# Sink keys of a windowed attention: zero-padded full-array matmuls for two heads at once, and one burst of row-tiled score matmuls per unit

## Chip, cores and metric

The kernel runs on one core of one Trainium2 chip. The metric is the device time of one execution in microseconds. A run is called slow when it took over 1.5% more than the fastest of the same kernel in its job, otherwise fast, and only fast runs are compared. Ratios are the mean time of one kernel's fast runs over that of the other's fast runs of the same rounds, so not quite the ratio of the medians that are quoted.

Words used here: PE is TensorE, PEld its weight loads, ACT ScalarE, DVE VectorE, POOL GpSimd. "Start to start" is the distance from the start of one matmul in the trace to the start of the next.

## The reference

Causal attention with a window of 128 keys plus 4 "sink" keys that every query sees, followed by a two-layer FFN.

```python
# B, H, S, D = 4, 8, 768, 64;  n_sink, window = 4, 128
scores = q @ k.T / sqrt(D)
keep = (pos_k < n_sink) | ((pos_q - pos_k >= 0) & (pos_q - pos_k < window))
a = softmax(where(keep, scores, -1e9))
x = (a @ v)  # reordered to (B*S, H*D) = (3072, 512)
h = x @ w_in                                   # 512 -> 2048
out = (h / (1 + exp(-beta * h))) @ w_out       # 2048 -> 512
```

## The kernel before

The program is a list of operations that a small scheduler in Python orders for each engine, with its own model of durations. A *unit* is half a sequence (384 queries) of a pair of heads; there are 32. For each unit: `T` transposes q and k, `SC` computes scores, exps and masks, `AV` multiplies with v (a 65th column of ones gives the denominator), `OT` transposes the result into `xT`. The FFN parts `H` (w_in, 4 matmuls of 384 columns) and `O` (w_out, 16 of 512 columns) fill the gaps.

Blocks of scores are 128 keys by 128 queries. Kinds: `d` diagonal, `p` the block before it, `s` block 0 where it holds both window and sinks, `k` the 4 sink keys alone, for queries too far away to see block 0 in their window. A head has 64 dimensions, so the two heads of a unit lie on rows 0 to 63 and 64 to 127 of the array, and their score matmuls run side by side as row tiles into different PSUM banks.

```python
GROUPS = [[[("s", 0, 0), ("s", 0, 1), ("d", 1, 1), ("p", 1, 2)], [("d", 2, 2), ("k", 0, 2)]],
          [[("d", 3, 3), ("p", 2, 3), ("p", 3, 4)], [("d", 4, 4), ("d", 5, 5), ("p", 4, 5)],
           [("k", 0, 3), ("k", 0, 4), ("k", 0, 5)]]]

def SC(u, j):                       # one group = one burst; two or three per unit
    bs = take(2)                    # two adjacent PSUM banks, one per head
    ...
        for hh in range(2):
            rows = slice(64 * hh, 64 * hh + 64)
            dst = bank[0:NSINK if sink else 128, ...]
            lhsT = kt[rows, 1, 0:NSINK] if sink else kt[rows, 1, kc:kc + 128]
            ... matmul(dst, lhsT, qkT[u % NT][rows, 0, ...])
    ... exp of all of both banks on ACT; masks on POOL and DVE

def AV(u):
    for m, ps in enumerate(parts(half)):        # three blocks of 128 queries
        for hh in range(2):
            for n, (kind, j, i, kb) in enumerate(ps):   # k (sinks) first, then p, d
                rows = slice(0, 128 if kb >= 0 else NSINK)
                ... matmul(A[:, c0:c0 + D + 1], E[z][rows, i, hh, :],
                           vaug[vz][rows, kb % NK, 2 * hp + hh, :], start=(n == 0), ...)
```

The sink scores fill 4 of 128 PSUM rows and the exp reads all 128, so VectorE clears PSUM once at the start (two memsets).

At the start q, k and v arrive per pair of heads. The k loads are issued on ACT's queue, in program order with ACT's casts.

```python
add("act" if hp is not None and n == "k" else "sp", lambda e, ...: e.dma_start(dst, src), ...)
...
LOADS = xl(0) + [0, 1, 2, 3] + xl(1) + [4, 5, 6, 7] + ...   # q,k,v of half 0; w_in; half 1; w_out; the rest
```

The softmax here doesn't subtract the row's maximum and nothing guards it: scores larger than these inputs give would overflow.

## Time and profile before

Median 290.97 us of three runs (289.66 to 291.53). The profiled execution took 287.25 us, its span from first to last instruction 285.5 us.

| | before |
|---|---|
| PE busy | 262.1 us, 92% |
| ACT, DVE, POOL busy | 60%, 45%, 34% |
| PE waiting for a named engine | 20.2 us in all, 15.8 of them for the first q and k casts |
| AV (480 matmuls): busy, its two shapes added / start to start | 62.7 us / 44.3 us |
| changes of array shape between neighbouring matmuls | 386 |

Lines of the profile's page: the busy time of each engine, and over 40 equal slices the busy share of PE and its granted clock in tenths.

```profile
PE 262.1 (92%) x1953; PEld 143.5 (50%) x1953; DVE 128.2 (45%) x252; ACT 172.4 (60%) x280; POOL 97.2 (34%) x192
PE   0249997989999999999999999999999999999995
PEclk9999999798999999999999999999999999999999
PE 86%; ACT 4%; DMA 4%; SPq 2%; DVE 1%; issue 1%; POOL 0%; DVEq 0%
```

The last line is the chain of waits, share of the span by engine. From the fourth slice on PE is busy for 70% or more of every slice but the last, mostly for over 90%, and the chain runs through it, so PE time saved there is mostly time saved. (The clock row misses the start: until 32.5 us w_in matmuls follow each other at 320 ns, and the transposes before them at 107 ns, twice what they take later, so PE ran at half speed there though the row shows 9.) PE's busy time cannot say how much is saved: matmuls overlap, and a matmul that is held up by its neighbour looks no different in its mean duration. The groups of AV by shape (count, then busy us and mean ns of one) show it:

```profile
L517 PE MATMUL P<-vaug,E 128*128 128x65 bf16 x352 | 37.0, 204 | 0.0
L517 PE MATMUL P<-vaug,E 4*128 4x65 bf16 x128 | 25.7, 201 | 0.4 <-ACT E L474 0.4
```

Both forms last about 200 ns. From the start times of all matmuls in the trace the picture differs. Medians, start to start:

```
128-row AV -> 128-row AV        38 ns
128-row AV -> 4-row AV         129 ns     4-row AV -> 128-row AV       131 ns
H -> H (384 columns)           163 ns     H -> row-tiled scores        258 ns
O -> O (512 columns)           216 ns     O -> row-tiled scores        312 ns
64x128 scores -> H             148 ns     128-column transpose -> same  56 ns
```

Every change of the array's shape adds 91 to 96 ns to the distance seen without it, whichever way. The weight loads show where it is lost: between two 128-row AV matmuls the second one's weight load starts 11 ns after the first matmul (median), but 125 ns after it where the shape changes, 4 ns before its own matmul.

The Trainium skill, "TensorEngine Tiling (Array Packing)", Key Properties, says: "Mode switching requires drain". It gives no time; this trace does.

### The profile page before, as it was taken

How to read it: one execution, taken by the hardware profiler on the slowest of the kernel's cores; microseconds unless marked ns; L12 is line 12 of the kernel's file. 1: busy time of each engine (PE TensorE's matmuls, PEld its weight loads, DVE VectorE, ACT ScalarE, POOL GpSimd, SP SyncE). 2: the span in 40 equal slices, each digit the busy share in tenths (PEclk: the TensorE clock that was granted, in tenths of full speed). 3: DMA queues.
4: the chain of work that ended last, by engine and by line, in shares of the span. 5: the costliest groups of instructions: out<-in, count | busy, mean ns of one | idle time of the engine just before them, and what ended most of it. 6: DMA issues, size and time to landing. Idle time of an engine off the chain costs nothing.

```text
span 285.5 us, 5121 instructions
## 1 busy us (share of the span) xinstructions
PE 262.1 (92%) x1953; PEld 143.5 (50%) x1953; DVE 128.2 (45%) x252; ACT 172.4 (60%) x280; POOL 97.2 (34%) x192
## 2 busy tenths in 40 slices
PE   0249997989999999999999999999999999999995
PEld 0125554444556555565556645555555555555542
DVE  5214694643466463533546523254353353353320
ACT  3359699424786776777867876555555465464430
POOL 2125066665295864949537335000000000000000
PEclk9999999798999999999999999999999999999999
DMA  6962998899999997741000101010010101101001
GB/s 137 279 210 89 307 240 288 240 276 225 275 240 253 229 254 189 181 115 39 1 3 1 39 0 39 0 39 37 37 39 37 65 13 42 68 0 76 37 37 73
DMA packets 82856, 33.89 MB, mean 119 GB/s; under 512 B 75648, under 2 KB 75664, under 8 KB 82832
## 3 DMA queue, kind: packets, MB, share of 16 engines
q1 hardware_dynamic: 79632, 32.78, 42.6%
q10 hardware_dynamic: 3200, 0.79, 1.2%
q8 instruction: 15, 0.25, 0.3%
q14 instruction: 9, 0.07, 0.1%
HBM read 27.27 MB, written 6.29 MB: 118 GB/s over the span
## 4 chain that ended last, share of the span: by engine, by line
PE 86%; ACT 4%; DMA 4%; SPq 2%; DVE 1%; issue 1%; POOL 0%; DVEq 0%
PE P L555 30%; PE P L573 30%; PE P L517 14%; PE P L467 6%; PE P L418 4%; DMA k_stage<-in_k_dram 3%; ACT E L474 2%; PE P L535 2%; SPq L349 2%; DMA q_stage<-in_q_dram 1%; ACT w_in L306 1%; DVE onorm L523 1%; ACT qkT L306 1%; ACT t L559 0%; DVE g L561 0%
## 5 line engine op out<-in xcount | busy, mean ns | idle before, releaser
L561 DVE SCALAR_TENSOR_TENSOR g<-t,P 128x384 bf16<-128x384 f32 x128 | 70.2, 554 | 94.0 <-ACT t L559 82.4
L559 ACT ACTIVATE t<-P,hbeta 128x384 f32<-128x384 f32 x128 | 73.8, 582 | 49.6 <-PE P L555 47.0
L555 PE MATMUL P<-xT,w_in 128*128 128x384 bf16 x512 | 100.8, 331 | 0.1
L573 PE MATMUL P<-w_out,g 128*128 128x512 bf16 x384 | 99.5, 385 | 0.5 <-DVE g L561 0.5
L474 ACT ACTIVATE E<-P 128x768 bf16<-128x768 f32 (+1 forms) x80 | 61.2, 817 | 19.3 <-PE P L467 19.2
L481 POOL TENSOR_SCALAR_AFFINE_SELECT E<-E 128x256 bf16<-128x256 bf16 (+1 forms) x112 | 54.7, 516 | 46.6 <-ACT E L474 46.6
L555 PEld LDWEIGHTS P<-xT,w_in 128*128 128x128 bf16 x512 | 48.5, 99 | 40.4 <-issue 4.6
L573 PEld LDWEIGHTS P<-w_out,g 128*128 128x128 bf16 x384 | 36.0, 99 | 36.3 <-issue 2.9
L517 PE MATMUL P<-vaug,E 128*128 128x65 bf16 (+1 forms) x480 | 46.5, 203 | 0.4 <-ACT E L474 0.4
L517 PEld LDWEIGHTS P<-vaug,E 128*128 128x128 bf16 (+1 forms) x480 | 31.6, 98 | 18.4 <-issue 3.2
L467 PE MATMUL P<-qkT 64*128 64x256 bf16 (+3 forms) x288 | 27.0, 266 | 1.3 <-ACT E L474 1.1
L306 ACT ACTIVATE osb<-P 128x512 f32<-128x512 f32 x22 | 13.1, 597 | 13.8 <-PE P L573 13.6
L306 ACT ACTIVATE xT<-P 128x384 bf16<-128x384 bf16 x26 | 12.6, 494 | 12.7 <-PE P L535 12.6
L489 DVE TENSOR_TENSOR E<-E,maskS 128x512 bf16<-128x512 bf16 x16 | 8.6, 537 | 23.1 <-ACT E L474 23.1
L467 PEld LDWEIGHTS P<-qkT 64*128 64x128 bf16 (+1 forms) x288 | 10.1, 91 | 17.2 <-issue 7.5
L523 DVE TENSOR_TENSOR onorm<-P,rden 128x384 bf16<-128x384 f32 x32 | 17.8, 557 | 1.1
L418 PE MATMUL P<-ident,k_0 128*128 128x128 bf16 x48 | 6.0, 241 | 10.6 <-POOL k_0 L405 10.6
L405 POOL TENSOR_SCALAR_AFFINE_SELECT vaug<-v_stage 128x512 bf16<-128x512 f32 x21 | 14.3, 679 | 3.8 <-DMA v_stage<-in_v_dram 2.4
L306 ACT ACTIVATE qkT<-P 128x768 bf16<-128x768 bf16 x14 | 11.0, 810 | 5.6 <-PE P L418 4.1
L405 POOL TENSOR_SCALAR_AFFINE_SELECT k_0<-k_stage 128x512 bf16<-128x512 f32 (+1 forms) x13 | 7.6, 584 | 17.4 <-DMA k_stage<-in_k_dram 17.4
L535 PE MATMUL P<-ident,onorm 128*128 128x128 bf16 x96 | 11.3, 233 | 1.8 <-DVE onorm L523 1.8
L521 DVE RECIPROCAL rden<-P 128x6 f32<-128x6 f32 x32 | 6.2, 193 | 14.8 <-PE P L517 14.7
(34 smaller groups left out, 98.0 us busy)
## 6 DMA issues: line engine op xcount, KB each, us to landing
out_dram<-osb SPq DMA_DIRECT2D x24, 256.0 KB, 2.0
q_stage<-in_q_dram SPq DMA_DIRECT2D x21, 256.0 KB, 4.3
k_stage<-in_k_dram SPq DMA_DIRECT2D x21, 256.0 KB, 4.3
v_stage<-in_v_dram SPq DMA_DIRECT2D x21, 256.0 KB, 4.3
wst<-in_moe_w_in_dram SPq DMA_DIRECT2D x4, 1024.0 KB, 6.8
wst<-in_moe_w_out_dram SPq DMA_DIRECT2D x4, 1024.0 KB, 6.7
q_stage<-in_q_dram SPq DMA_DIRECT2D x8, 96.0 KB, 2.7
v_stage<-in_v_dram SPq DMA_DIRECT2D x8, 96.0 KB, 2.7
```

Of the source, the lines that this page charges most:

```text
L306: return lambda e: e.activation(dst, src, AF.Copy, bias=0.0, scale=scale)
L405: fn = lambda e: e.affine_select(dst, src, patt, ALU.is_ge, 0.0, base=0, channel_multiplier=0)
L418: add("pe", lambda e, i=i, n=n, c=c: nc.tensor.transpose(mp[:, i * HALF + c * 128:i * HALF + (c + 1) * 128], x16[n][hb % NX][:, c, 2 * hp: ...
L467: add("pe", lambda e, dst=dst, lhsT=lhsT, rows=rows, q0=q0, nq=nq: e.matmul(dst, lhsT, qkT[u % NT][rows, 0, q0:q0 + 128 * nq].rearrange("p ...
L474: add("act", lambda e: e.activation(dst_, src, AF.Exp, bias=0.0, scale=SCALE), act_ns(256 * n), w=[(k_, z, j) for k_ in "Edps"], x=[("B", ...
L481: add("gp", lambda e, d=d, sg=sg, at_=at_: e.affine_select(d, d, [[0, 2 * len(at_)], [sg, 128]], ALU.is_ge, 0.0, base=min(sg, 0), channel_ ...
L517: e.matmul(A[:, c0:c0 + D + 1], E[z][rows, i, hh, :], vaug[vz][rows, kb % NK, 2 * hp + hh, :], start=a, stop=o), mm_ns(D + 1),
L523: add("dve", lambda e: e.tensor_tensor(onorm[on][:, :, :, :].rearrange("p m h d -> p (m h) d"), av[:, :, 0:D], rden[on][:, :].unsqueeze(2) ...
L555: add("pe", lambda e, c=c: e.matmul(hp, w_in16[:, c, m * 128:(m + 1) * 128], xT[:, c, t0:t0 + HALF], start=(c == 0), stop=(c == 3)), mm_ns ...
L559: add("act", lambda e: e.activation(tt[ti][:, :], hp, AF.Tanh, bias=0.0, scale=hbeta[:, m:m + 1]), act_ns(HALF) + 93, r=["hbeta"], w=[("t" ...
L561: add("dve", lambda e: e.scalar_tensor_tensor(gt[T_ % NG][:, m, :], tt[ti][:, :], 1.0, hp, ALU.add, ALU.mult), dve_ns(HALF), r=[("t", ti)] ...
L573: add("pe", lambda e, m=m: e.matmul(P[:, bk, :], gt[T_ % NG][:, m, t * 128:(t + 1) * 128], w_out16[:, m, :], start=(m == 0), stop=(m == NM ...
```

## The change

Its intent: no 4-row matmuls at all, and one row-tiled burst per unit instead of two or three. The sink keys of both heads are copied into one zero-padded stationary tile `kS` (head 0 in columns 0 to 3 of rows 0 to 63, head 1 in columns 32 to 35 of rows 64 to 127), so one full-array matmul `SS` gives both heads' sink scores. The sink values go into `vS`, zero but for rows 0 to 3 (head 0) and 32 to 35 (head 1). A zero score has exp 1, but its row of `vS` is zero. One 130-column matmul then starts the accumulation of both heads.

```diff
-    GROUPS = [[[s0, s1, d1, p(1,2)], [d2, k2]],           [[d3, p3, p4], [d4, d5, p5], [k3, k4, k5]]]
+    GROUPS = [[[s0, s1, d1],         [d2, p(1,2)]],       [[d3, p3, p4], [d4, d5, p5]]]
-    def SC(u, j):                     +    def SC(u):
-        bs = take(2)                  +        bs = take(4)        # both groups, four adjacent banks
...                                    # all matmuls of both groups, then both exps
+        G.free["pe"] += 190           # the scheduler's model learns what a burst costs
+    def SS(u):
+        ... matmul(P[:, bs[0], q0:HALF], kS[ks][:, :], qkT[u % NT][:, 0, q0:HALF])
+        ... exp -> ES[z]
     def AV(u):
         for m, ps in enumerate(parts(half)):
+            far = NK * half + m >= 2
+            if far:
+                matmul(A[:, c0:c0 + 2 * (D + 1)], ES[z][:, m * 128:(m + 1) * 128],
+                       vS[b % 2][:, 2 * hp:2 * hp + 2, :], start=True, stop=False)
             for hh in range(2):
-                    rows = slice(0, 128 if kb >= 0 else NSINK)
-                    ... mm_ns(D + 1)
+                    ... start=(n == 0 and not far) ... 39     # ns in the scheduler's model
     def T(u):       # in the first half of each sequence
+        kS[ks][rows, 32 * hh:32 * hh + NSINK] <- k's first 4 columns in PSUM, for each head
     def cast(...):
+        vS[z][32 * hh:32 * hh + NSINK, ...] <- vaug, on DVE
     def consts():
+        memsets of kS and vS on POOL
-        two memsets of PSUM on DVE
```

(The diff is abridged: block names are shortened, bookkeeping of the scheduler is left out.)

More of the change, by code (lines that the diff above doesn't have):

```diff
@@ L229, in _program @@
     NU = 2 * NPAIR
-    NSTG, NX, NV, NT, NE, NON, NG, NTT, NOS, NWS = 2, 2, 3, 8, 3, 3, 3, 3, 3, 2
+    NSTG, NX, NV, NT, NE, NON, NG, NTT, NOS, NWS, NKS = 2, 2, 3, 8, 3, 3, 3, 3, 3, 2, 4
     NK = NB // 2
@@ L245, in _program @@
     qkT = sb("qkT", (128, 2, HALF), BF16, NT)
-    E = sb("E", (128, 9, 2, 128), BF16, NE)
+    E = sb("E", (128, 6, 2, 128), BF16, NE)
+    ES = sb("ES", (128, HALF), BF16, NE)
+    kS = sb("kS", (128, 128), BF16, NKS)
+    vS = sb("vS", (128, H, D + 1), BF16, 2)
     onorm = sb("onorm", (128, NK, 2, D), BF16, NON)
@@ L316, in consts @@
             add("gp", lambda e, i=i: e.memset(vaug[i][:, :, :, D:D + 1], 1.0), 50, w=[("vones", i)])
+        for i in range(NKS):
+            add("gp", lambda e, i=i: e.memset(kS[i][:, :], 0.0), 80, w=[("kS", i)])
+        for i in range(2):
+            add("gp", lambda e, i=i: e.memset(vS[i][:, :, :], 0.0), 350, w=[("vS", i)])
         for i, sg in ((0, 1), (1, -1)):
@@ L323, in consts @@
             r=[("maskS0", 0), ("maskS0", 1)], w=["maskS"])
-        for h in range(2):
-            add("dve", lambda e, h=h: e.memset(P[:, 4 * h:4 * h + 4, :], 0.0), 2200,
-                x=[("B", i) for i in range(4 * h, 4 * h + 4)])
     def beta_in():
@@ L408, in cast @@
         add(eng, fn, opts[eng], r=r, w=w)
+        if n == "v" and hb % 2 == 0 and (hp == 3 or c == 0):
+            z = hb // 2 % 2
+            v0 = vaug[hb % NV][0:NSINK, 0, :, :].rearrange("p (a two) d -> p a two d", two=2)
+            for hh in range(2):
+                dst_ = vS[z][32 * hh:32 * hh + NSINK, :, :].rearrange("p (a two) d -> p a two d", two=2)[:, :, hh, :]
+                add("dve", lambda e, dst_=dst_, hh=hh: e.tensor_copy(dst_, v0[:, :, hh, :]), 200,
+                    r=[("vS", z)] + [("v", hb % NV, 0, j) for j in range(4)], w=[("vSd", z, hh)])
     def T(u):
@@ L425, in T @@
             w=[("qkT", u % NT)], x=[("B", bs[0])])
+        if hb % 2 == 0:
+            ks = u % NKS
+            for hh in range(2):
+                rows = slice(64 * hh, 64 * hh + 64)
+                add(eng, copy_fn(eng, kS[ks][rows, 32 * hh:32 * hh + NSINK], mp[rows, HALF:HALF + NSINK]), 70,
+                    r=[("kS", ks)], w=[("kSd", ks, hh)], x=[("B", bs[0])])
         give(bs)
-    GROUPS = [[[("s", 0, 0), ("s", 0, 1), ("d", 1, 1), ("p", 1, 2)], [("d", 2, 2), ("k", 0, 2)]],
-              [[("d", 3, 3), ("p", 2, 3), ("p", 3, 4)], [("d", 4, 4), ("d", 5, 5), ("p", 4, 5)],
-               [("k", 0, 3), ("k", 0, 4), ("k", 0, 5)]]]
+    GROUPS = [[[("s", 0, 0), ("s", 0, 1), ("d", 1, 1)], [("d", 2, 2), ("p", 1, 2)]],
+              [[("d", 3, 3), ("p", 2, 3), ("p", 3, 4)], [("d", 4, 4), ("d", 5, 5), ("p", 4, 5)]]]
     def slots(half):
@@ L442, in slots, with SC @@
         return out_
-    def SC(u, j):
+    def SC(u):
         b, half, hp = where(u)
         z = u % NE
-        bs = take(2)
-        grp = GROUPS[half][j]
-        n = len(grp)
-        s0 = slots(half)[grp[0]][1]
-        jobs = {}
-        for i, (kind, kb, qb) in enumerate(grp):
-            jobs.setdefault((kb, kind == "k"), []).append((qb, i))
-        for (kb, sink), cols in jobs.items():
-            cols.sort()
-            own = u if kb >= NK * half else u - 4
-            kt = qkT[own % NT]
-            kc = (kb % NK) * 128
-            q0, i0, nq = (cols[0][0] - NK * half) * 128, cols[0][1], len(cols)
-            st = cols[1][1] - i0 if nq > 1 else 1
-            for hh in range(2):
-                rows = slice(64 * hh, 64 * hh + 64)
-                bank = P[:, bs[hh], :].rearrange("p (s w) -> p s w", w=128)
-                dst = bank[0:NSINK if sink else 128, i0:i0 + st * (nq - 1) + 1:st, :]
-                lhsT = kt[rows, 1, 0:NSINK] if sink else kt[rows, 1, kc:kc + 128]
-                add("pe", lambda e, dst=dst, lhsT=lhsT, rows=rows, q0=q0, nq=nq: e.matmul(
-                    dst, lhsT, qkT[u % NT][rows, 0, q0:q0 + 128 * nq].rearrange("p (s w) -> p s w", w=128),
-                    start=True, stop=True), mm_ns(128 * nq) / 2,
-                    r=[("qkT", u % NT), ("qkT", own % NT)], x=[("B", bs[hh])])
-        step = bs[1] - bs[0]
-        src = P[:, bs[0]:bs[1] + 1:step, 0:128 * n].rearrange("p h (s w) -> p h s w", w=128)
-        dst_ = E[z][:, s0:s0 + n, :, :].rearrange("p s h w -> p h s w")
-        add("act", lambda e: e.activation(dst_, src, AF.Exp, bias=0.0, scale=SCALE), act_ns(256 * n),
-            w=[(k_, z, j) for k_ in "Edps"], x=[("B", i) for i in bs])
-        give(bs)
-        for kind, sg in (("d", 1), ("p", -1)):
-            at_ = [i for i, blk in enumerate(grp) if blk[0] == kind]
-            if at_:
-                d = E[z][:, s0 + at_[0]:s0 + at_[-1] + 1, :, :].rearrange("p s h w -> p (s h) w")
-                add("gp", lambda e, d=d, sg=sg, at_=at_: e.affine_select(
-                    d, d, [[0, 2 * len(at_)], [sg, 128]], ALU.is_ge, 0.0, base=min(sg, 0), channel_multiplier=-sg),
-                    pool_ns(256 * len(at_), 2 * len(at_)), r=[("E", z, j)], w=[(kind, z, j)])
-        if grp[0][0] == "s":
-            d = E[z][:, s0:s0 + 2, :, :]
-            mask = maskS[:, :, :].unsqueeze(2).to_broadcast([128, 2, 2, 128])
-            opts = {"gp": 1150, "dve": dve_ns(512)}
-            eng = quickest(opts)
-            add(eng, lambda e: e.tensor_tensor(d, d, mask, ALU.mult), opts[eng], r=[("E", z, j), "maskS"],
-                w=[("s", z, j)])
@@ new lines, in SC @@
+        bs = take(4)
+        for j, grp in enumerate(GROUPS[half]):
+            jobs = {}
+            for i, (kind, kb, qb) in enumerate(grp):
+                jobs.setdefault(kb, []).append((qb, i))
+            for kb, cols in jobs.items():
+                cols.sort()
+                own = u if kb >= NK * half else u - 4
+                kt = qkT[own % NT]
+                kc = (kb % NK) * 128
+                q0, i0, nq = (cols[0][0] - NK * half) * 128, cols[0][1], len(cols)
+                st = cols[1][1] - i0 if nq > 1 else 1
+                for hh in range(2):
+                    rows = slice(64 * hh, 64 * hh + 64)
+                    bank = P[:, bs[2 * j + hh], :].rearrange("p (s w) -> p s w", w=128)
+                    dst = bank[:, i0:i0 + st * (nq - 1) + 1:st, :]
+                    add("pe", lambda e, dst=dst, kt=kt, kc=kc, rows=rows, q0=q0, nq=nq: e.matmul(
+                        dst, kt[rows, 1, kc:kc + 128],
+                        qkT[u % NT][rows, 0, q0:q0 + 128 * nq].rearrange("p (s w) -> p s w", w=128),
+                        start=True, stop=True), mm_ns(128 * nq) / 2,
+                        r=[("qkT", u % NT), ("qkT", own % NT)], x=[("B", bs[2 * j + hh])])
@@ new lines, in SC @@
+        G.free["pe"] += 190
+        for j, grp in enumerate(GROUPS[half]):
+            n, s0 = len(grp), slots(half)[grp[0]][1]
+            src = P[:, bs[2 * j]:bs[2 * j] + 2, 0:128 * n].rearrange("p h (s w) -> p h s w", w=128)
+            dst_ = E[z][:, s0:s0 + n, :, :].rearrange("p s h w -> p h s w")
+            add("act", lambda e, src=src, dst_=dst_: e.activation(dst_, src, AF.Exp, bias=0.0, scale=SCALE),
+                act_ns(256 * n), w=[(k_, z, j) for k_ in "Edps"], x=[("B", i) for i in bs[2 * j:2 * j + 2]])
+            for kind, sg in (("d", 1), ("p", -1)):
+                at_ = [i for i, blk in enumerate(grp) if blk[0] == kind]
+                if at_:
+                    d = E[z][:, s0 + at_[0]:s0 + at_[-1] + 1, :, :].rearrange("p s h w -> p (s h) w")
+                    add("gp", lambda e, d=d, sg=sg, at_=at_: e.affine_select(
+                        d, d, [[0, 2 * len(at_)], [sg, 128]], ALU.is_ge, 0.0, base=min(sg, 0), channel_multiplier=-sg),
+                        pool_ns(256 * len(at_), 2 * len(at_)), r=[("E", z, j)], w=[(kind, z, j)])
+            if grp[0][0] == "s":
+                d = E[z][:, s0:s0 + 2, :, :]
+                mask = maskS[:, :, :].unsqueeze(2).to_broadcast([128, 2, 2, 128])
+                opts = {"gp": 1150, "dve": dve_ns(512)}
+                eng = quickest(opts)
+                add(eng, lambda e, d=d, mask=mask: e.tensor_tensor(d, d, mask, ALU.mult), opts[eng],
+                    r=[("E", z, j), "maskS"], w=[("s", z, j)])
@@ new lines, in SC @@
+        give(bs)
+    def SS(u):
+        b, half, hp = where(u)
+        z, ks = u % NE, (u - 4 * half) % NKS
+        q0 = 0 if half else 256
+        bs = take(1)
+        add("pe", lambda e: e.matmul(P[:, bs[0], q0:HALF], kS[ks][:, :], qkT[u % NT][:, 0, q0:HALF], start=True,
+                                     stop=True), mm_ns(HALF - q0),
+            r=[("kSd", ks, 0), ("kSd", ks, 1), ("qkT", u % NT)], x=[("B", bs[0])])
+        add("act", lambda e: e.activation(ES[z][:, q0:HALF], P[:, bs[0], q0:HALF], AF.Exp, bias=0.0, scale=SCALE),
+            act_ns(HALF - q0), w=[("ES", z)], x=[("B", bs[0])])
+        give(bs)
@@ L492, in parts @@
     def parts(half):
         sl = slots(half)
-        return [[("E" if blk[0] == "k" else blk[0], sl[blk][0], sl[blk][1], -1 if blk[0] == "k" else blk[1])
-                 for blk in sorted(sl, key=lambda x: "kspd".index(x[0])) if blk[2] == qb]
+        return [[(blk[0], sl[blk][0], sl[blk][1], blk[1])
+                 for blk in sorted(sl, key=lambda x: "spd".index(x[0])) if blk[2] == qb]
                 for qb in range(NK * half, NK * half + NK)]
@@ L501, in av_keys @@
         ks = {(p[0], z, p[1]) for ps in parts(where(u)[1]) for p in ps}
-        return sorted(ks) + [("v", u // 4 % NV, c, u % 4) for c in range(NK)]
+        return sorted(ks) + [("v", u // 4 % NV, c, u % 4) for c in range(NK)] + [("ES", z), ("vSd", u // 8 % 2, 1)]
     def AV(u):
@@ L509, in AV @@
         for m, ps in enumerate(parts(half)):
+            far = NK * half + m >= 2
+            if far:
+                c0 = 2 * m * (D + 1)
+                add("pe", lambda e, m=m, c0=c0: e.matmul(
+                    A[:, c0:c0 + 2 * (D + 1)], ES[z][:, m * 128:(m + 1) * 128],
+                    vS[b % 2][:, 2 * hp:2 * hp + 2, :].rearrange("p h d -> p (h d)"), start=True, stop=False,
+                    skip_group_check=True), mm_ns(2 * (D + 1)),
+                    r=[("ES", z), ("vSd", b % 2, 0), ("vSd", b % 2, 1)], x=[("B", bs[0])])
             for hh in range(2):
@@ L512, in AV @@
                 for n, (kind, j, i, kb) in enumerate(ps):
-                    rows = slice(0, 128 if kb >= 0 else NSINK)
-                    kb = max(kb, 0)
                     vz = (u if kb >= NK * half else u - 4) // 4 % NV
-                    add("pe", lambda e, c0=c0, hh=hh, i=i, kb=kb, vz=vz, rows=rows, a=(n == 0), o=(n == len(ps) - 1):
-                        e.matmul(A[:, c0:c0 + D + 1], E[z][rows, i, hh, :], vaug[vz][rows, kb % NK, 2 * hp + hh, :],
-                                 start=a, stop=o), mm_ns(D + 1),
+                    add("pe", lambda e, c0=c0, hh=hh, i=i, kb=kb, vz=vz, a=(n == 0 and not far), o=(n == len(ps) - 1):
+                        e.matmul(A[:, c0:c0 + D + 1], E[z][:, i, hh, :], vaug[vz][:, kb % NK, 2 * hp + hh, :],
+                                 start=a, stop=o, skip_group_check=True), 39,
                         r=[(kind, z, j), ("v", vz, kb % NK, hp)], x=[("B", bs[0])])
@@ L585, in OQ @@
                 dma=f"do{z}")
-    done = {s: 0 for s in ("cast", "T", "SC", "AV", "OT", "H", "O", "load", "W")}
+    done = {s: 0 for s in ("T", "SC", "SS", "AV", "OT", "H", "O", "load")}
     def xl(hb):
@@ L595, in _program @@
     LOADS = xl(0) + [0, 1, 2, 3] + xl(1) + [4, 5, 6, 7] + [x for hb in range(2, NSB) for x in xl(hb)]
-    SCS = [(u, j) for u in range(NU) for j in range(2 if where(u)[1] == 0 else 3)]
-    n_sc = [0] * (NU + 1)
     CASTS = [x for hb in range(NSB) for x in xl(hb)]
@@ L601, in _program @@
     n_cast, n_w = [0], [0]
-    def units_sc():
-        i = done["SC"]
-        return NU if i == len(SCS) else SCS[i][0]
     def head(s):
@@ L611, in head @@
         if s == "T":
-            if i >= NU or i - NT + 4 >= units_sc():
+            if i >= NU or i - NT + 4 >= min(done["SC"], done["SS"]):
                 return None
@@ L618, in head @@
             fn = lambda: (T(i), mark(("qkTu", i), ("qkT", i % NT)))
-        elif s == "SC":
-            if i >= len(SCS):
-                return None
-            u, j = SCS[i]
-            if u >= done["AV"] + NE:
-                return None
-            t, tb = G.at([("qkTu", u)]), banks_at(2)
-            fn = lambda: SC(u, j)
+        elif s in ("SC", "SS"):
+            if i >= NU or i >= done["AV"] + NE:
+                return None
+            t, tb = G.at([("qkTu", i)]), banks_at(4 if s == "SC" else 1)
+            fn = lambda: (SC if s == "SC" else SS)(i)
         elif s == "AV":
-            if i >= NU or i >= done["OT"] + NON or i >= units_sc() or n_cast[0] < (3 * i + 3 if i < 4 else 12 + 9 * (i // 4)):
+            if i >= NU or i >= done["OT"] + NON or i >= min(done["SC"], done["SS"]) or n_cast[0] < (3 * i + 3 if i < 4 else 12 + 9 * (i // 4)):
                 return None
@@ L714, in _program @@
         best = None
-        for s in ("OT", "AV", "SC", "T") + ffn:
+        for s in ("OT", "AV", "SC", "SS", "T") + ffn:
             h = head(s)
@@ L744, in _program @@
         done[s] += 1
-        if s in "HO":
+        if s in ("H", "O"):
             last = s
```

## The prediction

> **What bounds the kernel.** TensorE. The engine table has PE busy 92% of a 285.5 us span (ACT 60%, DVE 45%, POOL 34%), the chain of waits is 86% PE, and the table of waits shows about 20 us of PE waiting, 16 of them for the first q and k casts before 21 us. From 80 us to the end the stretch view shows PE without gaps. So what PE saves there is saved in the span.
>
> **What an instruction costs.** Busy means (203 ns for an AV matmul) are latencies; I use start-to-start distances of neighbouring matmuls. FFN: 162 ns (384 columns) and 216 ns (512). AV matmul following AV matmul, both 128 rows: 38 ns. AV going into a 4-row sink matmul: 129 ns; out of it: 131 ns. A row-tiled score burst is entered about 95 ns late and left about 92 ns late. So each change of array shape costs about 92 ns. This agrees with the Trainium skill, "TensorEngine Tiling (Array Packing)", Key Properties: "Mode switching requires drain".
>
> **Removed and added on PE.**
> 1. AV: 128 four-row sink matmuls go (2 per first-half unit, 6 per second-half unit). 64 full-array matmuls of 130 columns come, about 57 ns each (estimate from the 56 ns of 128-column transposes), without a shape change. 128 x (93 + 91 + 38) ns - 64 x 57 ns = about 25 us.
> 2. Scores: all bursts cost 30.5 us over the surrounding work, about 25 without stalls and cold clock. Afterwards: 32 bursts of about 475 ns (first half) or 527 ns (second half, such a burst was measured) = 16 us, plus 16 x 57 + 16 x 162 ns of full-array sink scores = 3.5 us. Saves 5 to 6 us.
> Together 30 to 31 us of PE work.
>
> **Other engines.** Exps: 1024+512 columns become 768+512+128, and 3x768 becomes 768+768+384, so ACT falls by a few us. Small copies (32 for kS, 8 for vS) and six POOL memsets come: off the critical path, though kS copies hold the transposes' bank longer. Two PSUM memsets of 1.76 us leave DVE.
>
> **What is on the path.** Before about 50 us DMA and casts set the pace (DMA share about 1 in 30 to 50 us; PE waits for k casts, then has only FFN-in work), so the saving of the first four to six units is largely hidden: minus 3 to 4 us. On the other hand, without the memsets DVE is free for the first q cast; in the trace ACT issues the first k load only at 4.2 us, after its own q cast. I expect k loads earlier, and 1 to 3 us gained in start-up. Bursts needing four adjacent free banks beside the FFN's banks may delay scores and make ACT waits: minus 1 to 2 us.
>
> Net saving about 29 us: **262 us**, range 255 to 269. Chances: faster by over 2% 0.95, within 2% 0.03, slower 0.02.
>
> **What would show it.** Start-to-start inside AV is 38 ns throughout, with about 57 ns for the sink matmul; AV falls from 47 us of PE stream to about 19 to 22. Score bursts number about 32 instead of 50 groups of 80 bursts. FFN distances stay 162 and 216 ns. ACT exp falls from 61 to about 57 us. PE waits after 50 us stay under 4 us. Attention work ends at about 155 us instead of 178; what follows is FFN only. The first k cast comes before 7.7 us.
>
> **What would make it wrong.** The four-bank requirement starves scores, so that PE runs out of FFN work; ACT (over 75% busy during attention) becomes the limit; start-up reorders for the worse; or zero-padded matmuls pace slower than 57 ns because of their weight loads.

## More of the kernel before

The timeline (start us, duration us, instructions merged) shows a whole AV of a second-half unit and its neighbours:

```profile
95.64 1.86 PE L517 MATMUL P<-vaug,E 4*128 4x65 bf16 x18
97.44 0.32 PE L467 MATMUL P<-qkT 64*4 64x384 bf16 x2
97.69 0.82 PE L555 MATMUL P<-xT,w_in 128*128 128x384 bf16 x4
```

18 matmuls take 97.44 - 95.64 = 1.80 us, 100 ns each. Six of them are sinks, each between two 128-row matmuls.

## The result

Median 261.62 us (259.92 to 262.38, four runs) against 290.83 us (289.66 to 291.53) for the kernel before in the same rounds: ratio 0.899, 95% interval 0.893 to 0.905. The forecast of 262 us holds. The span of the profiled execution is 260.7 us, 24.8 us less than before. The timed difference is 29.2 us, because the profile of before fell on one of its quicker executions and that of the changed kernel on its slowest (262.38 us). The clock is part of it: in a later job the fast runs of before with a granted clock of 0.994 took 286.15 and 286.83 us, and those with 0.982 and 0.976 took 289.15 and 290.19 us. In the two later jobs 12 of the 14 runs of before had 0.982 or less, while the changed kernel's eight runs had 0.991 to 1.0. By the distance between those two pairs of times, an estimate, some 3 us of the timed gain are fewer stretches at half speed; whether fewer changes of shape bring that about, no run separates.

The same lines of the page after:

```profile
PE 228.8 (88%) x1861; PEld 132.3 (51%) x1889; DVE 129.0 (49%) x285; ACT 166.5 (64%) x302; POOL 96.7 (37%) x197
PE   1307899669999999999999999999999999999995
PEclk9999999799999999999999999999999999999999
PE 68%; DMA 10%; ACT 9%; DVE 7%; SPq 2%; issue 2%; POOL 1%; DVEq 0%
```

PE records 1861 matmuls against 1889 weight loads: 28 matmuls of O are missing from this trace (28 x 216 ns = 6.0 us), so its busy time reads too low. The chain of waits is now 68% PE instead of 86%: other engines have come onto it. AV by shape:

```profile
L552 PE MATMUL P<-vaug,E 128*128 128x65 bf16 x352 | 20.6, 201 | 1.2 <-POOL E L496 0.4 <-ACT E L490 0.3 <-ACT xT L309 0.2
L542 PE MATMUL P<-vS,ES 128*128 128x130 bf16 x64 | 13.4, 229 | 0.0
```

And the timeline of one AV of a second-half unit (the sink matmuls have their own line now):

```profile
93.11 0.23 PE L542 MATMUL P<-vS,ES 128*128 128x130 bf16 x1
93.17 0.28 PE L552 MATMUL P<-vaug,E 128*128 128x65 bf16 x4
93.29 0.22 PE L542 MATMUL P<-vS,ES 128*128 128x130 bf16 x1
93.35 0.28 PE L552 MATMUL P<-vaug,E 128*128 128x65 bf16 x4
93.47 0.22 PE L542 MATMUL P<-vS,ES 128*128 128x130 bf16 x1
93.53 0.28 PE L552 MATMUL P<-vaug,E 128*128 128x65 bf16 x4
93.65 0.22 PE L514 MATMUL P<-qkT,kS 128*128 128x128 bf16 x1
```

93.65 - 93.11 = 0.54 us for what took 1.80 us before. The duration of one matmul is still about 200 ns; only the distance between starts has changed: 57 ns after a sink matmul, 29 ns after a 65-column one.

Where the span went can be added up from the start times. Each matmul gets its distance in an undisturbed sequence (H 162, O 216, transpose 56, AV 30 ns and so on). What a change of shape adds to that is taken as measured, at most 110 ns each. AV matmuls between two changes also follow each other at 38 instead of 29 ns; this is a line of its own. What is left is waiting and cold clock. The 28 missing matmuls are put back.

| from the first to the last matmul, us | before | after | difference |
|---|---|---|---|
| undisturbed matmuls | 210.3 | 209.1 | -1.2 |
| changes of shape (386, then 62) | 38.3 | 6.1 | -32.2 |
| slower AV between two changes | 1.2 | 0.3 | -0.9 |
| rest: until the first FFN matmul | 16.9 | 20.0 | +3.1 |
| rest: from there to 63 us | 6.5 | 9.2 | +2.7 |
| rest: from 63 us to the end of attention | 2.7 | 6.2 | +3.5 |
| rest: FFN alone | 0.9 | 0.9 | 0 |
| sum | 276.8 | 251.8 | -25.0 |

The work of the array is the same. The change removes 324 changes of shape, which with their slower neighbours were 33 us, 100 ns for each; and about 9 us came back as waiting.

The waits of PE after 50 us (who waited for whom: total us, times, longest), first before, then after (without four entries of 0.2 to 0.3 us), show some of what came back:

```profile
PE P L535 <- DVE onorm L523: 0.9, 1, 0.9
PE P L573 <- DVE g L561: 0.5, 2, 0.3
```

```profile
PE P L570 <- DVE onorm L558: 2.8, 7, 0.9
PE P L608 <- ACT w_out L309: 1.6, 2, 1.3
PE P L608 <- DVE g L596: 0.5, 2, 0.3
PE P L608 <- issue: 0.5, 3, 0.2
```

PE now comes to a unit's last transposes before VectorE has normalised the result, and to the first O before w_out has been cast.

### The profile page after: what moved, and what is told of

Its sections match the earlier page's. It is cut to its first block, busy times and chain, and to the rows that moved or that the text cites. A ratio compares the mean times of both kernels' runs of the same rounds, so it can differ in the third digit from the quotient of the medians.

```text
span 260.7 us, 5023 instructions
## 1 busy us (share of the span) xinstructions
PE 228.8 (88%) x1861; PEld 132.3 (51%) x1889; DVE 129.0 (49%) x285; ACT 166.5 (64%) x302; POOL 96.7 (37%) x197
## 4 chain that ended last, share of the span: by engine, by line
PE 68%; DMA 10%; ACT 9%; DVE 7%; SPq 2%; issue 2%; POOL 1%; DVEq 0%
PE P L590 30%; PE P L608 28%; DMA wst<-in_moe_w_out_dram 6%; ACT E L490 4%; DMA k_stage<-in_k_dram 3%; PE P L480 3%; DVE onorm L558 2%; SPq L353 2%; PE P L429 2%; PE P L570 2%; PE P L552 2%; DVE g L596 2%; ACT t L594 2%; DMA v_stage<-in_v_dram 1%; DVE qkT L307 1%
## 5 line engine op out<-in xcount | busy, mean ns | idle before, releaser
L608 PE MATMUL P<-w_out,g 128*128 128x512 bf16 x356 | 93.2, 381 | 6.3 <-DVE w_out L308 2.3
L490 ACT ACTIVATE E<-P 128x768 bf16<-128x768 f32 x64 | 45.0, 770 | 4.0 <-PE P L480 3.7
L552 PE MATMUL P<-vaug,E 128*128 128x65 bf16 x352 | 20.6, 201 | 1.2 <-POOL E L496 0.4
L309 ACT ACTIVATE osb<-P 128x512 f32<-128x512 f32 x22 | 13.2, 599 | 12.9 <-PE P L608 12.8
L552 PEld LDWEIGHTS P<-vaug,E 128*128 128x128 bf16 x352 | 17.8, 102 | 5.0 <-POOL E L496 1.4
L480 PE MATMUL P<-qkT 64*128 64x128 bf16 (+1 forms) x256 | 16.8, 254 | 0.8 <-ACT E L490 0.8
L517 ACT ACTIVATE ES<-P 128x128 bf16<-128x128 f32 (+1 forms) x32 | 11.7, 398 | 6.0 <-PE P L514 5.8
L429 PE MATMUL P<-ident,k_0 128*128 128x128 bf16 x48 | 6.0, 241 | 8.7 <-DVE k_0 L307 8.7
L480 PEld LDWEIGHTS P<-qkT 64*128 64x128 bf16 x256 | 9.1, 99 | 8.7 <-issue 3.2
L542 PE MATMUL P<-vS,ES 128*128 128x130 bf16 x64 | 13.4, 229 | 0.0
L429 PE MATMUL P<-ident,q_0 128*128 128x128 bf16 x48 | 6.0, 241 | 7.1 <-DVE q_0 L307 5.3
L570 PEld LDWEIGHTS P<-ident,onorm 128*128 128x128 bf16 x96 | 6.7, 100 | 9.7 <-DVE onorm L558 5.2
```

What stands on the lines that cost most here:

```text
L309: return lambda e: e.activation(dst, src, AF.Copy, bias=0.0, scale=scale)
L429: add("pe", lambda e, i=i, n=n, c=c: nc.tensor.transpose(mp[:, i * HALF + c * 128:i * HALF + (c + 1) * 128], x16[n][hb % NX][:, c, 2 * hp: ...
L480: add("pe", lambda e, dst=dst, kt=kt, kc=kc, rows=rows, q0=q0, nq=nq: e.matmul(dst, kt[rows, 1, kc:kc + 128], qkT[u % NT][rows, 0, q0:q0 + ...
L490: add("act", lambda e, src=src, dst_=dst_: e.activation(dst_, src, AF.Exp, bias=0.0, scale=SCALE), act_ns(256 * n), w=[(k_, z, j) for k_ i ...
L552: e.matmul(A[:, c0:c0 + D + 1], E[z][:, i, hh, :], vaug[vz][:, kb % NK, 2 * hp + hh, :], start=a, stop=o, skip_group_check=True), 39,
L570: add("pe", lambda e, m=m: nc.tensor.transpose(mp[:, m * 128:(m + 1) * 128], onorm[on][:, m, :, :].rearrange("p h d -> p (h d)"), ident[:, ...
```

## The experiments

Theory 1: on a saturated PE each change of array shape costs about 92 ns (the forecast's figure; the sum above has 100), and their removal is the gain. Rivals: the gain is in merging the heads' matmuls (fewer instructions), in the single burst, or in the freed VectorE at the start. All variants start from the changed kernel, and all gave right results.

### Shape without merging, merging without shape

`sink_merged_64rows`: the contraction of the merged sink matmul is cut from 128 to 64 rows. The rows cut off are zeros. The instructions on each engine are the same and in the same order.

```diff
-  A[:, c0:c0 + 2 * (D + 1)], ES[z][:, m * 128:(m + 1) * 128], vS[b % 2][:, 2 * hp:2 * hp + 2, :]
+  A[:, c0:c0 + 2 * (D + 1)], ES[z][0:64, m * 128:(m + 1) * 128], vS[b % 2][0:64, 2 * hp:2 * hp + 2, :]
```

> The changed kernel with one size altered: the 64 sink AV matmuls read rows 0 to 63 of ES and vS instead of 0 to 127 (the rows left out are zeros, the result stays right). Same instructions in the same order on every engine. Theory 1 (each change of array shape costs about 92 ns on a saturated PE): 64 entries and 64 exits, 64 x 184 ns = 11.8 us of PE stream, of which 9 to 12 us reach the time: about 272 us. Rival (what counted was that two matmuls of 65 columns became one of 130): no difference, about 262 us.

`sink_two_full`: two matmuls of 65 columns, one per head, each still with 128 rows.

```diff
-  if far: matmul(A[:, 130 columns], ES[z][:, ...], vS[b % 2][:, 2 * hp:2 * hp + 2, :], start=True)
   for hh in range(2):
+      if far: matmul(A[:, c0:c0 + D + 1], ES[z][rows, ...], vS[b % 2][rows, 2 * hp + hh, :], start=True)   # rows = 0:128
```

> The changed kernel with each merged sink AV matmul split in two, one per head, still full-array: 128 of 65 columns instead of 64 of 130. Theory 1: 128 x 29 ns = 3.7 us against 64 x 57 ns = 3.6 us, so no difference, about 262 us. Rival (the merging of heads was the gain): several us slower.

`sink_two_64rows`: the same with `rows = 0:64`.

> The changed kernel with 128 sink AV matmuls, one per head, each reading 64 rows, so that each is entered and left by a change of array shape, as in the kernel before. Theory 1: 128 x 184 ns = 23.6 us of PE stream, of which 19 to 24 us reach the time: about 283 us, and about twice the loss of the merged 64-row version. Rival (merging): the same loss as the split full-array version.

| sink matmuls | shape changes they add | median us | mean of fast runs us | against the split full-array version |
|---|---|---|---|---|
| 128 of 65 columns, 128 rows | 0 | 260.50 | 260.05 | |
| 64 of 130 columns, 64 rows | 128 | 266.74 | 267.04 | +7.0 |
| 128 of 65 columns, 64 rows | 256 | 282.79 | 282.71 | +22.7 |
| kernel before, same rounds | | 289.31 | 289.43 | |

The split full-array version stands at ratio 0.898 to the kernel before (0.892 to 0.904); the changed kernel had 0.899. (One of its five runs, the profiled one, was slow.) So merging the heads is worth nothing here, and 64 more matmuls did not matter. The two-times-64-row version loses 22.7 us, what was foretold (19 to 24 us); against the kernel before, its ratio of 0.977 (0.969 to 0.985) is "unclear" by the 2% rule of the record. In its trace the distances of the kernel before are back, 129 ns into a sink matmul and 133 ns out of it. AV start to start sums to 44.3 us, as before; after the change it was 20.6 us.

The merged 64-row version lost 7.0 us where 9 to 12 were expected (5.7 us against the changed kernel itself, whose runs are of another job). The changes of shape are there; the timeline shows 160 ns after a 130-column matmul where the changed kernel had 60:

```profile
87.41 0.23 PE L542 MATMUL P<-vS,ES 64*128 64x130 bf16 x1
87.57 0.30 PE L552 MATMUL P<-vaug,E 128*128 128x65 bf16 x4
87.80 0.23 PE L542 MATMUL P<-vS,ES 64*128 64x130 bf16 x1
```

AV's stream grew from 20.6 to 30.6 us, 10.0 us. But PE waited less. Its waits after 50 us:

```profile
PE P L570 <- DVE onorm L558: 1.3, 2, 0.9
PE P L608 <- DVE g L596: 0.5, 2, 0.3
PE P L608 <- issue: 0.5, 3, 0.2
PE P L608 <- ACT E L490: 0.2, 1, 0.2
```

The seven waits for `onorm` became two and the wait for w_out's cast on ACT is gone. The program order is the same, so this is the reverse of what the change did: a slower PE meets its inputs ready. The same sum as in the result's table, against a second run of the changed kernel (`after_again`, below, in another job):

| us | changed kernel again | merged, 64 rows | two, 64 rows |
|---|---|---|---|
| changes of shape and slower AV | 6.5 | 19.4 | 33.1 |
| rest (waiting and cold clock) | 34.0 | 27.2 | 32.6 |
| span | 257.9 | 264.2 | 282.8 |

The merged version adds 12.9 us of drains and saves 6.8 us of waiting, which leaves 6.1 of the 6.3 us by which its span grew. In the profile of the third version the rest fell by 1.4 us only; but it holds 10.2 us of half-speed clock (one window of 3.4 us at 48.5 us, one of 6.8 us at 62.1 us), where the other two have none from 36 us to their last microsecond, so its waiting is lower than the rest says. An estimate from these numbers: 26.6 us of drains more, 7 us of waiting less and 5 us lost to half speed make 24.6 us, and the span grew by 24.9. So by this estimate about 7 us of PE's time in the changed kernel are slack that a slower PE fills, and what exceeds it costs time. The loss of 22.7 us, too, holds some half speed: its fast runs had clocks of 0.976 to 0.988, those of the split full-array version 1.0.

### The single burst

`split_bursts`: each unit's two score groups are scheduled apart again, each with two banks; the sinks stay full-array.

```diff
-    def SC(u):                 +    def SC(u, only):          # only group `only`
-        bs = take(4)           +        bs = take(2) used twice
-   t, tb = ..., banks_at(4)    +   t, tb = ..., banks_at(2)  # two steps of the scheduler per unit
```

> The changed kernel with each unit's score burst split again into two, each taking two banks and scheduled alone; sinks stay full-array. If the burst's saving is on the path: 32 more entries and exits of the row-tiled shape, 32 x 187 ns = 6 us, so about 266 to 268 us. Rival (the saving was hidden in waits, and four adjacent banks cost waits of their own): 260 to 263 us, with fewer PE waits between 63 and 155 us.

Median 264.20 us (263.65 to 265.32), ratio 0.913 (0.907 to 0.919): 4.3 us slower than the split full-array version of the same job, in means of fast runs. It lies between the two expectations, and its trace fits neither. The first assumed 32 bursts more, but the scheduler often put groups back to back again: the scores form 39 unbroken stretches instead of 30, with 80 changes of shape in all instead of 62. At 100 ns each that is 1.8 us. The rival expected fewer waits of PE between 63 and 155 us, but they rose from 3.0 to 6.1 us, the longest (1.7 us) for a `qkT`. So less than half of the 4.3 us are changes of shape; the rest is most likely waiting, from another order of work, and no run separates its causes. With two banks for each step attention ends earlier: the last AV matmul starts 146.0 us after the span's start, with four banks at 156.8 and 154.1 us in the two profiles of the changed kernel. That did not shorten the whole, because H and O fill the time. Together with `sink_two_64rows`, which has all of the change but the AV part and is 6.7 us faster than the kernel before (289.43 - 282.71), this gives a rough account of the timed gain: about 23 us from the shape of the AV sink matmuls (with the half speed named above), and 6 to 7 us from the rest, of which about 4 go when each unit's scores are scheduled in two steps.

### The start

A second job, on another chip, with the changed kernel itself as yardstick. Against the kernel before, the record calls all four runs of this job "unclear" at 2%, where runs of before lie from 286.15 to 292.35 us in two states; the comparisons here are with the changed kernel in the same job.

> The changed kernel once more, unaltered, as the yardstick for the runs of this chip: 259 to 263 us.

> The changed kernel with the two PSUM memsets of 1.76 us on VectorE put back at the start (their results are not needed any more). The forecast said that their removal frees VectorE for the first q cast, brings the k loads forward and gains 1 to 3 us. If so: 1 to 3 us slower than the changed kernel, with the first FFN matmul later than 30.8 us. Rival (the start ends with the fourth k load, which queues behind the weight loads either way, so nothing was gained): within 1 us of the changed kernel, first FFN matmul between 30 and 32 us.

`memsets_back` puts the old PSUM memsets back:

```diff
+        for h in range(2):
+            add("dve", lambda e, h=h: e.memset(P[:, 4 * h:4 * h + 4, :], 0.0), 2200, ...)
```

| | median us | mean of fast runs us | first FFN matmul at us | last k cast of the first half at us |
|---|---|---|---|---|
| changed kernel again | 262.15 | 261.66 | 30.1 | 17.63 |
| memsets back | 261.21 | 261.01 | 30.0 | 20.58 |
| k_first | 257.28 | 256.76 | 25.9 | 10.48 |
| k_first_x1_early | 256.70 | 256.58 | 25.9 | 10.05 |
| kernel before, same rounds | 290.19 | 288.08 | | |

With the memsets the first casts go back to other engines and the last k cast comes 3 us later, yet the FFN starts at the same moment and the time is the same. So the removal of the memsets gave nothing, and the last k cast alone does not set the start either. In the changed kernel ACT and DVE cast w_in at 20.0 us, ahead of the first exps into E; with the memsets back they do so at 24.5 us, behind them. That may be what takes the lead away again; no run separates it. (The ratio of the changed kernel is 0.908 in this job, interval 0.899 to 0.918, because three of the seven runs of before count as slow here and are left out.)

`k_first` issues the eight k loads before any cast on ACT:

```diff
-    LOADS = xl(0) + [0, 1, 2, 3] + xl(1) + ...
+    LOADS = sorted(xl(0), key=lambda x: x[1] != "k") + [0, 1, 2, 3] + xl(1) + ...
```

> The changed kernel with the eight first k loads issued on ScalarE's queue before any cast that waits on that engine; TensorE's order is the same. If the last k load (its cast at 18.3 us, PE waiting 6.0 us for it) holds the start: last k cast before 13 us, first FFN matmul at 24 to 28 us, and the time 1 to 4 us shorter, less than the start gains because the w_out loads still arrive no earlier than about 45 us. Rival (the w_in loads and casts hold the start): first FFN matmul stays at 30 to 31 us and the time within 1 us.

4.9 us shorter (means of fast runs; one of its four runs, 260.05 us, counts as slow), more than the 1 to 4 us expected, and the first FFN matmul 4.2 us earlier, as expected. In the changed kernel ACT issues the last k load only when a cast before it has its data, at 9.5 us, next to the first w_in load at 9.7 us, and its cast comes at 17.6 us. The waits for k casts are gone from the table of `k_first`; in the changed kernel they were the largest entry (its first profile):

```profile
PE P L429 <- DVE k_0 L307: 8.7, 3, 6.0
```

`k_first` moved the last k cast by 7 us and the first w_in cast from 20.0 to 15.8 us, so it shows that the order of the loads holds the start, and not which of the two casts does.

`k_first_x1_early` also puts the second half's q, k, v ahead of the third and fourth w_in load:

```diff
-    ... + [0, 1, 2, 3] + xl(1) + [4, 5, 6, 7] + ...
+    ... + [0, 1] + xl(1) + [2, 3, 4, 5, 6, 7] + ...
```

> As k_first, and the q, k and v loads of the second half-sequence go ahead of the third and fourth w_in loads, which wait for a free staging buffer and so leave the DMA queue idle between 20 and 30 us (DMA share 0.55 there). Expected if PE's waits before 63 us are waits for data: DMA share over 0.8 between 20 and 30 us, the first transposes of the second half before 38 us instead of at 42.9, and 4 to 8 us shorter than the changed kernel, 253 to 258 us. Rival (ScalarE's exps and casts hold that phase): within 2 us of k_first.

256.70 us (255.60 to 257.33), within 1 us of `k_first`, as the rival had it. The time alone cannot decide, since 253 to 258 us had been expected of the other case; but against `k_first` nothing was gained, although the second half's first transposes came at 31.7 us instead of 37.2. Stretches of 10 us (busy us and count of PE, PEld, DVE, ACT, POOL; clock; DMA share; GB/s) of the changed kernel's first profile, then of this version:

```profile
20.00:30.00 10.00, 8.06 (x88) 4.99 (x88) 7.39 (x19) 8.96 (x16) 6.21 (x12) 1.00 0.55 181
30.00:40.00 10.00, 9.65 (x52) 5.41 (x51) 6.37 (x13) 7.12 (x13) 3.39 (x6) 1.00 0.91 218
40.00:50.00 10.00, 7.71 (x66) 4.18 (x65) 7.16 (x13) 7.51 (x14) 5.13 (x8) 0.90 0.83 271
```

```profile
20.00:30.00 10.00, 8.06 (x57) 4.75 (x56) 5.18 (x12) 5.21 (x10) 7.89 (x15) 1.00 1.10 300
30.00:40.00 10.00, 9.57 (x75) 5.66 (x74) 6.07 (x11) 9.26 (x17) 0.67 (x2) 1.00 0.47 178
40.00:50.00 10.00, 7.86 (x80) 3.84 (x79) 7.07 (x14) 9.75 (x16) 4.97 (x10) 1.00 0.78 274
```

The DMA queue is full between 20 and 30 us as intended (share 1.10 instead of 0.55; `k_first` alone had 0.91), and then is half idle between 30 and 40 us. PE is no busier. ACT is at 9.3 and 9.8 of 10 us from 30 to 50 us and may be the limit of that phase. The postponed w_in loads are a rival: the third and fourth are cast from 33.5 and 37.0 us, in `k_first` from 22.6 and 27.9 us. No run separates the two.

The fast runs of both versions beat all runs of both kernels in this job. The shorter one, 256.70 us, has ratio 0.891 to the kernel before (0.883 to 0.899); its slowest run was quicker than the quickest run of the changed kernel in the same job (257.33 against 259.65 us).

## Why the prediction was right

Time and direction held: 261.62 us for a forecast of 262. The mechanism and its largest term held too; smaller terms were off, and their errors cancelled in part.

- *"each change of array shape costs about 92 ns"*: shown, and a little more. 324 changes fewer are 33 us of PE's stream, 100 ns each with the slower AV matmuls around them. Adding 256 back, with the result unchanged, costs 22.7 us, some of it half speed.
- *AV saves "about 25 us"*: measured over the work around it, AV fell from 47.7 to 22.6 us, 25.1 us. Its detail was off: I forecast 38 ns between AV matmuls, as in the kernel before, and in the changed kernel the median is 29 ns. The 38 ns belonged to the short runs between two changes of shape.
- *Scores save "5 to 6 us"*: the row-tiled bursts fell from 30.5 to 21.1 us, and full-array sink scores of 3.5 us (undisturbed) came, 5.9 us less together. In the trace the sink scores have waits around them and their stream is 9.7 us, so as a raw sum scores did not shrink. The runs give 6 to 7 us for everything but the AV part, and do not show that the single burst saves its share by fewer changes of shape: `split_bursts` had only 18 more.
- *"minus 3 to 4 us" hidden early and "minus 1 to 2 us" of new waits*: too small. The traces show 9.3 us, of which 5.8 us before 63 us and 3.5 us during attention.
- *"1 to 3 us gained in start-up"*: wrong. The first k cast came earlier (5.03 us instead of 7.75), but the first FFN matmul came at 30.8 us instead of 30.5, and putting the memsets back changed nothing. I took the first wait in the list for the one that held the stage.
- *"PE waits after 50 us stay under 4 us"*: wrong. The table of waits after 50 us sums to 6.5 us, against 1.4 us before.
- *"Attention work ends at about 155 us"*: 156.8 us. *"ACT exp falls from 61 to about 57 us"*: 45.0 us for E and 11.7 us for ES, 56.7 us. *"Score bursts number about 32"*: 30 groups in the trace, one of them three bursts back to back.

By the traces alone the saving is 24.8 us and not the 29 us forecast; the timed saving is 29.2 us. The forecast took a saving read from the profile off the timed median of before (290.97 us), while that profile was of an execution of 287.25 us. Its own terms add up to 25 to 30 us, so 29 stood near their upper end. So part of the close agreement is luck: waits that were underrated by about 4 us, and a start that gained nothing, against a clock that was higher after the change.

## What to carry to other kernels

Price matmuls by the distance between starts, pair by pair of neighbouring shapes; a sink matmul of 4 rows and 65 columns has a duration like any other, and cost about 184 ns beyond its own slot of 38 ns, by the two drains around it. On this saturated PE a small contraction between full-array matmuls was cheaper padded with zeros to the full array; a row-tiled burst has to pay for its entry and exit, some 190 ns together (how long it must be for that, no run here tests). Once PE is faster, look again at what it waits for: here 9 of 33 us came back as waits, and issuing eight loads earlier regained about 5 us. And count in the trace what a variant really did: `split_bursts` was meant to add 64 changes of shape and added 18.

## What the Trainium skill lacked or had wrong

- "TensorEngine Tiling (Array Packing)", Key Properties: it says that a mode switch drains the array, without a time. Here a change adds 91 to 102 ns each way at full clock (the upper figure if AV's slot is taken as 29 ns and not 38), for 128 rows to 64 and 128 rows to 4; a change from 128 to 4 columns inside row-tiled scores costs about the same (146 to 156 instead of 53 ns).
- "TensorEngine Tiling (Array Packing)", When to Use Tiling: it recommends row tiling by the contraction alone (64 or less, 32 or less) and does not set the cost of the mode switch against it. For a lone matmul between full-array ones the full array was the better choice here: padding 64 sink matmuls from 64 to 128 rows gained about 7 us, and 128 of them 22.7 us.
- "TensorE: Matmul & The Clock Gate", Back-to-back issue gap: it gives about 81 ns (128 columns) and 131 ns (512 columns) for streams of weight load and matmul, and says that its formula of columns / 2.4 + 2.5 ns is for isolated matmuls and misjudges streams. These traces show 56 ns for 128 columns, 216 ns for 512 and 29 ns for 65, each matmul with its own weight load: the formula holds in the stream, as the page's own Part 1 has it for 128 and 512 columns.
- "TensorE: Matmul & The Clock Gate", Part 4: it says that the full clock does not engage for transposes. Here 128-column transposes among FFN matmuls follow each other at 56 ns, the distance of 128 columns at full clock, where each lasts about 220 to 240 ns. So they do run at full clock once it is granted. Before the FFN starts they follow at 107 ns; whether transposes alone would bring the full clock, no run here tests.
